# Loading the last 224 rows of w_out: five 108-partition chunks by transfers over three DMA engines, in place of nine 44-partition chunks over eight, five, three and three

## The chip, the cores and the metric

The kernel runs on one core of a Trainium2 chip. A core has five engines that run side by side: TensorE (PE in the profile, its weight loads PEld), VectorE (DVE), ScalarE (ACT), GpSimd (POOL) and SyncE (SP), which issues most transfers. Sixteen DMA engines move the data between the chip's main memory and the on-chip memory of 128 partitions. The metric is the device time of one execution in microseconds (us); lower is better. Times below are medians over several runs; a profile describes one execution.

## What is computed

A decode step of one token for four sequences: layer normalization, then attention over a cache of 4,096 positions in 32 heads, and beside it a gated feed-forward branch, both added to the input. Cut to what matters:

```python
B, Sq, D = 4, 1, 640;  H, Sk, Dh = 32, 4096, 128;  Fh = 864     # bf16
x = A_x
xn = _layernorm(x)
# A: attention over the cache
q = (xn @ wq).reshape(B, Sq, H, Dh).transpose(0, 2, 1, 3)
p = softmax(einsum('bhqd,bhkd->bhqk', q, k_cache) * Dh ** -0.5)
A = einsum('bhqk,bhkd->bhqd', p, v_cache).transpose(0, 2, 1, 3).reshape(B, Sq, H * Dh) @ wo
# B: gated feed-forward
z = gelu(xn @ w_in)                        # w_in: 640 x 1728
z1, z2 = z[..., :Fh], _layernorm(z[..., Fh:])
g = w_sp * z2 + b_sp                       # S = 1: two scalars
Bout = (z1 * g) @ w_out                    # w_out: 864 x 640
return x + A + Bout
```

The two caches are 134 MB each and are read once. All weights together are about 14 MB.

## The kernel before

One large tile, `kv`, holds five slots of equal size, and nearly everything that comes from main memory goes through them. A unit is one (head group, sequence) pair of K or of V: 128 partitions x 65,536 bytes, 8 MB, over two half slots. There are 16 units of K and 16 of V. `seq` gives their order (four K first, then V and K by turns), `place` their slots. SP issues them with `load_unit` (L167) one unit ahead of the computation; a load waits until the slot's earlier readers are done.

Before the units SP issues, in this order: wq (L111), w_in (L114), the first part of w_out (L118) and the rest of w_out (L128). ScalarE's queue issues three tiny ones, w_sp, b_sp (L107, L108) and x (L105). Each transfer raises a counter when it lands; there are eight counters, used in turn in the order of the program, so the ninth transfer of the program waits until the first has landed, and so on. Here the transfers in order are w_sp, wq, b_sp, x, w_in, w_out, and then the small ones.

W_out has 864 rows of 640 bf16 values. The first `nf = FA * P` = 512 rows lie in `kv` as four chunks of 128 partitions. The other 352 rows lie in two tiles of the pool `ktpool`, `w_rest0` with seven chunks and `w_rest1` with two, on 44 partitions (`NRP`). They come in four transfers, listed in `RB` as (partition block of 32, first chunk, i, chunks): 32 partitions with 7 rows each, 20 with 1, 12 with 7 and 12 with 2. `w_rest1` is cleared first (L123, GpSimd), because its partitions aren't all loaded. In the two small tiles' transfers the outer dimension of the source is i (8, 5, 3 and 3). The pool `ktpool` has two buffers, which the transposed K tiles `kT` use later.

The branch B at the start: L287 makes q from wq; L309 and L312 make z, the first part into `z_ps`, the rest into `zr_ps`; ScalarE's L318 and L322 apply gelu and put z in the order of the chunks; L335 to L352 normalize and gate it; L353 transposes it to `uT`, one block of 32 columns for each chunk; and L367 multiplies chunk after chunk with w_out and adds the products to `proj`, where the attention's output joins them later (L517).

The loop over the units: `emit_K` transposes K in 32x32 blocks on VectorE (L389, eight pieces per unit) and multiplies with the zero-padded query (L400). After four units `softmax` follows, and `z_fill` lays the probabilities out for V. `emit_V` multiplies with V (L474, 64 matmuls per unit). At the end wo's last parts are loaded (L175), the last piece of wo in four cuts, and L517 to L583 finish the projection, add the partial sums and store.

Python runs all loops when the program is built, and the Tile framework puts the waits in. Within each engine the instructions run in the order written out.

Of the kernel before, what the change touches and what calls it, by code (L numbers as in the profile page):

```python
# [11 lines left out]
F32 = mybir.dt.float32  # L12
BF16 = mybir.dt.bfloat16
# [3 lines left out]
def kernel(  # L17
# [19 lines left out]
    nc = tc.nc  # L37
    P = 128
    B, Sq, D = A_x.shape
    _, H, Sk, Dh = A_k_cache.shape  # L40
    assert Sq == 1 and B == 4 and Dh == P and D % P == 0
    DC = D // P
# [6 lines left out]
    TC = 32  # L49
# [4 lines left out]
    G = HG * B  # L54
    F2 = B_w_in.shape[1]
    Fh = F2 // 2
    FA = 4
    FR = 9
    RB = ((0, 0, 8, 7), (0, 7, 5, 1), (1, 0, 3, 7), (1, 7, 3, 2))
    NRP = 44  # L60
    assert Fh == FA * P + 4 * sum(i * c for _, _, i, c in RB)
    FC = FA + FR
    NOUT = A_wo.shape[1]
    NH = 2
    NO2 = NOUT // NH
# [3 lines left out]
    const = ctx.enter_context(tc.tile_pool(name="const", bufs=1))  # L69
    small = ctx.enter_context(tc.tile_pool(name="small", bufs=2))  # L70

    NKT = max(2 * TC * 32, 7 * NOUT // 2)
    ktpool = ctx.enter_context(tc.tile_pool(name="ktpool", bufs=2))
    ppool = ctx.enter_context(tc.tile_pool(name="ppool", bufs=2))
    ps_s = ctx.enter_context(tc.tile_pool(name="ps_s", bufs=1, space=bass.MemoryType.PSUM))
# [7 lines left out]
    def misc_ps(shape, dtype):  # L83
        misc_ctr[0] += 1
        return ps_m.tile(shape, dtype, tag="misc", name=f"misc{misc_ctr[0]}")
# [5 lines left out]
    def at_slot(i, n, off=0):  # L91
        return kv[:, i * SL + off:i * SL + off + n]
# [22 lines left out]

    nf = FA * P
    w_out = at_slot(2, FA * NOUT, n_in).rearrange("p (c n) -> p c n", c=FA)
    nc.sync.dma_start(out=w_out, in_=B_w_out[0:nf, :].rearrange("(p c) n -> p c n", p=P))  # L118
    w_rest = []
    for k, n in ((0, 7), (1, 2)):  # L120
        t = ktpool.tile([P, NKT], F32, tag="kT", name=f"w_rest{k}")[:NRP].bitcast(BF16)[:, 0:n * NOUT]
        w_rest.append(t.rearrange("p (c n) -> p c n", c=n))
    nc.gpsimd.memset(w_rest[1].rearrange("p c n -> p (c n)").bitcast(F32), 0.0)  # L123
    r_at = [nf]
    for q, c0, ni, n in RB:
        r_at.append(r_at[-1] + 4 * ni * n)
        k = c0 // 7
        nc.sync.dma_start(out=w_rest[k][32 * q:32 * q + 4 * ni, 0:n].rearrange("p c n -> p (c n)"),  # L128
                          in_=B_w_out[r_at[-2]:r_at[-1], :].rearrange("(r i c) n -> i r (c n)", r=4, c=n))

    NB = 32 * FC
    z_at = n_in + FA * NOUT

# [18 lines left out]
    def unit(item, t0, t1):  # L152

        s0, s1 = place[item]
        assert s1 == s0 + 1 or t1 <= T // 2 or t0 >= T // 2
        if t0 >= T // 2:
            return at_slot(s1, (t1 - t0) * Dh, t0 * Dh - SL)
        return at_slot(s0, (t1 - t0) * Dh, t0 * Dh)
# [47 lines left out]
    xnT = const.tile([P, DC, 32], BF16)  # L206
# [43 lines left out]
    for q in range(4):  # L250
        nc.gpsimd.tensor_copy(out=SelE[32 * q:32 * q + 32, :, q % 2, :],
                              in_=b8[32 * q:32 * q + 32, 8:8 + HP, None].to_broadcast((32, HP, P // HG)))
# [10 lines left out]
                          in_=ident_f[:].rearrange("p (q x c) -> p q x c", q=2, c=C2))  # L263
# [12 lines left out]
    for hf in range(NH):  # L276
        nc.tensor.matmul(proj[0:32, 0:NO2], lhsT=ident_bf[:XR, 1 - hf:33 - hf],
                         rhs=x_bf[:, hf * NO2:(hf + 1) * NO2], start=(hf == 0), stop=False)
# [4 lines left out]
    for hf in range(2):  # L283
        for c in range(DC):
            for j in range(NG):
                n0 = j * HG * Dh + hf * 512
                nc.tensor.matmul(q4_ps[32 * j:32 * j + 32, hf * 512:hf * 512 + 512], lhsT=xnT[:, c, :],  # L287
                                 rhs=wq[:, c, n0:n0 + 512], start=(c == 0), stop=(c == DC - 1))
# [13 lines left out]

    w_z = w_in.rearrange("p c (a f) -> p c a f", a=2)
    z_ps = misc_ps([P, 2, FA, 32], F32)
    zr_ps = misc_ps([64, 2, 256], F32)
    w_za = w_z[:, :, :, 0:nf].rearrange("p c a (q j i) -> p c q a i j", q=4, j=32)
    for c in range(DC):
        for q in range(4):
            nc.tensor.matmul(z_ps[32 * q:32 * q + 32], lhsT=xnT[:, c, :], rhs=w_za[:, c, q], start=(c == 0), stop=(c == DC - 1))  # L309
        for q in range(2):  # L310
            f0, f1 = r_at[2 * q], r_at[2 * q + 2]
            nc.tensor.matmul(zr_ps[32 * q:32 * q + 32, :, 0:f1 - f0], lhsT=xnT[:, c, :],  # L312
                             rhs=w_z[:, c, :, f0:f1], start=(c == 0), stop=(c == DC - 1))
    z_f = at_slot(2, 2 * 3 * NB, z_at).bitcast(F32).rearrange("p (a n) -> p a n", a=3)
    z_b = at_slot(2, 2 * NB, z_at + 6 * NB).rearrange("p (a n) -> p a n", a=2)
    zT = z_f[:, 0:2, :].rearrange("p a (i j) -> p a i j", j=32)
    nc.gpsimd.memset(z_f[:, 0:2, :], 0.0)
    nc.scalar.activation(out=zT[:, :, 0:FA, :], in_=z_ps[:], func=ACT.Gelu_apprx_tanh)  # L318
    for (q, c0, ni, n), f0, f1 in zip(RB, r_at[:-1], r_at[1:]):
        f0, f1 = f0 - r_at[2 * q], f1 - r_at[2 * q]  # L320
        for a in range(2):
            nc.scalar.activation(out=zT[32 * q:32 * q + 32, a, FA + c0:FA + c0 + n, 0:4 * ni].rearrange("p c (i r) -> p c i r", r=4),  # L322
                                 in_=zr_ps[32 * q:32 * q + 32, a, f0:f1].rearrange("p (r i c) -> p c i r", r=4, c=n),
                                 func=ACT.Gelu_apprx_tanh)

    one_bf = const.tile([1, P], BF16)
# [34 lines left out]
    for f0 in range(0, FC, 4):  # L361
        for hf in range(NH):
            for fc in range(f0, min(f0 + 4, FC)):
                n = P if fc < FA else NRP
                nb = 32 if fc == 1 and hf == 0 else RW
                u0, r0 = 32 * fc + 1 - hf, 32 * (fc % 2)
                nc.tensor.matmul(proj[r0:r0 + nb, 0:NO2], lhsT=uT[:n, u0:u0 + nb],  # L367
                                 rhs=(w_out[:, fc] if fc < FA else w_rest[(fc - FA) // 7][:, (fc - FA) % 7])[:, hf * NO2:(hf + 1) * NO2],
                                 start=(fc == 1 and hf == 0), stop=False)


# [9 lines left out]
    def emit_K(u, k):  # L381
# [5 lines left out]
        kw = unit(("k", u), t0, t0 + 2 * TC).bitcast(F32).rearrange("p (t w) -> p t w", w=KW)[:, :, 32 * kh:32 * kh + 32]  # L387
        kT = ktpool.tile([P, NKT], F32, tag="kT", name="kT")[:, 0:2 * TC * 32]
        nc.vector.transpose(kT[:].rearrange("p (t r) -> p t r", r=32), kw)  # L389
# [171 lines left out]
    for c, hf in ((0, 0), (1, 0), (0, 1), (1, 1), (2, 0), (2, 1)):  # L561
        p = min(c, 1)
# [49 lines left out]
```

## Time and profile before

| what | value |
|---|---|
| time, median of 3 runs (663.18 to 663.21) | 663.18 us |
| span of the profiled execution | 661.2 us |
| TensorE busy | 287.5 us, 43% |
| VectorE busy | 372.2 us, 56% |
| ScalarE busy | 73.6 us, 11% |
| GpSimd busy | 67.0 us, 10% |
| read from main memory | 282.24 MB, 427 GB/s over the span |
| packets of the DMA queues | 6930 |

The span counts from the first instruction of the program to the last; what the time holds besides is 2.0 us. An engine is busy while it works on data; waiting and issuing transfers don't count. In the DMA part of the page each digit is the busy share of one fortieth of the span, in tenths. The queue q1 is SP's, q10 ScalarE's; q8 and q14 fetch instructions. The chain of waits goes from the last instruction backwards, at each step to what released it.

The issues of the transfers around the change, with sizes and the median time from issue to landing:

```profile
kv<-in_A_wq_dram SPq DMA_DIRECT2D x1, 5120.0 KB
...
kv<-in_B_w_in_dram SPq DMA_DIRECT2D x1, 2160.0 KB, 19.8
...
kv<-in_B_w_out_dram SPq DMA_DIRECT2D x1, 640.0 KB, 20.9
...
w_rest<-in_B_w_out_dram SPq DMA_DIRECT2D x1, 280.0 KB
...
w_rest<-in_B_w_out_dram SPq DMA_DIRECT2D x1, 105.0 KB
w_rest<-in_B_w_out_dram SPq DMA_DIRECT2D x1, 30.0 KB
w_rest<-in_B_w_out_dram SPq DMA_DIRECT2D x1, 25.0 KB
```

And SP's own timeline up to the first loads of K (start, duration, what):

```profile
1.62 0.46 SPq L118 DMA_DIRECT2D kv<-in_B_w_out_dram  x1
2.12 14.46 SPq L128 DMA_DIRECT2D w_rest<-in_B_w_out_dram  x4
16.62 37.98 SPq L167 DMA_DIRECT2D kv<-in_A_k_cache_dram  x3
```

### The profile page before, as it was taken

To read this page: it belongs to the slowest core of one execution; us is meant where nothing else is said; L and a number is where in the kernel's file an instruction comes from. 1 tells how busy PE (TensorE), PEld (TensorE's weight loads), DVE (VectorE), ACT (ScalarE), POOL (GpSimd) and SP (SyncE) were. 2 spreads that over 40 slices of the span, in tenths; PEclk is the share of its full clock that TensorE was granted. 3 is DMA by queue.
4 is the path that set the end of the run, shared out by engine and by line. 5 is a ranking of instruction groups with operands and counts; after the bars stand their busy time and mean duration, and the time that the engine had idled before them with its cause. 6 is when DMAs were issued, how large, how long until landed. Compare 5 with 4: busy or idle time off the path is not lost.

```text
span 661.2 us, 5415 instructions
## 1 busy us (share of the span) xinstructions
PE 287.5 (43%) x2247; PEld 106.6 (16%) x2247; DVE 372.2 (56%) x306; ACT 73.6 (11%) x145; POOL 67.0 (10%) x137
## 2 busy tenths in 40 slices
PE   0436656446062555235436065533706244551236
PEld 0211212112011121111112022110202112120113
DVE  2229999766191759718356286764629175971112
ACT  0300000341100000430200000070110000043200
POOL 3600000031200000130300000030110000003300
PEclk9857788669577587676758577875858769766678
DMA  9999999999999999999999999999999999999996
GB/s 372 452 446 420 420 447 438 429 444 417 436 436 433 428 425 437 433 436 445 416 432 433 432 421 450 427 432 429 437 440 433 424 433 416 445 444 429 419 420 285
DMA packets 6930, 282.58 MB, mean 427 GB/s; under 512 B 811, under 2 KB 1091, under 8 KB 1487
## 3 DMA queue, kind: packets, MB, share of 16 engines
q1 hardware_dynamic: 6879, 282.24, 99.0%
q8 instruction: 17, 0.28, 0.2%
q14 instruction: 6, 0.05, 0.0%
q10 hardware_dynamic: 28, 0.01, 0.0%
HBM read 282.24 MB, written 0.01 MB: 427 GB/s over the span
## 4 chain that ended last, share of the span: by engine, by line
DMA 77%; DVE 9%; issue 8%; PE 4%; ACT 0%; SPq 0%; DVEq 0%; ACTq 0%
DMA kv<-in_A_k_cache_dram 46%; DMA kv<-in_A_v_cache_dram 26%; DVE kT L389 8%; PE O L474 4%; DMA kv<-in_A_wo_dram 4%; DMA kv<-in_A_wq_dram 2%; DVE pT_t L456 0%; ACT Zb L437 0%; DVE m L407 0%; ACT p_bf L450 0%; PE S L400 0%; PE misc L411 0%; SPq L128 0%; PE proj L517 0%; DVE o_q L569 0%
## 5 line engine op out<-in xcount | busy, mean ns | idle before, releaser
L389 DVE STREAM_TRANSPOSE kT<-kv 128x2048 f32<-128x2048 f32 x128 | 282.8, 2275 | 128.1 <-DMA kv<-in_A_k_cache_dram 128.1
L400 PE MATMUL S<-kT,QZ 128*32 128x512 bf16 x1024 | 187.1, 498 | 261.9 <-DVE kT L389 261.9
L400 PEld LDWEIGHTS <-QZ 128*32 128x32 bf16 x1024 | 59.8, 110 | 387.5 <-issue 323.2
L474 PE MATMUL O<-kv,Zb 128*32 128x512 bf16 x1024 | 75.0, 458 | 56.4 <-DMA kv<-in_A_v_cache_dram 49.5
L437 ACT ACTIVATE Zb<-pT_t,MkE 32x128 bf16<-32x128 bf16 x120 | 60.8, 507 | 117.6 <-PE O L474 104.6
L483 DVE TENSOR_TENSOR om<-O,Mk 128x512 f32<-128x512 f32 x15 | 10.4, 692 | 93.8 <-PE O L474 93.8
L435 POOL TENSOR_SCALAR Zb<-pT_t,MkE 32x128 bf16<-32x128 bf16 x60 | 43.1, 718 | 138.6 <-PE O L474 126.1
L474 PEld LDWEIGHTS <-Zb 128*32 128x32 bf16 x1024 | 34.0, 113 | 97.3 <-issue 69.6
L450 ACT ACTIVATE p_bf<-S,negmax 128x1024 bf16<-128x1024 f32 x4 | 4.5, 1115 | 403.7 <-DVE negmax L417 403.7
L433 DVE TENSOR_SCALAR Zb<-pT_t,MkE 32x128 bf16<-32x128 bf16 x76 | 25.1, 330 | 2.3
L375 POOL COPY QZ<-qT 32x32 bf16<-32x32 bf16 x16 | 5.0, 315 | 188.9 <-PE S L400 188.4
L484 DVE TENSOR_REDUCE R<-om 128x128 f32<-128x512 f32 x15 | 15.3, 1021 | 0.5
L456 DVE STREAM_TRANSPOSE pT_t<-p_bf 128x1024 bf16<-128x1024 bf16 (+1 forms) x8 | 9.6, 1240 | 5.5 <-ACT p_bf L450 5.5
L461 POOL TENSOR_SCALAR rs<-MkB,rowsum 128x4 f32<-128x4 f32 x4 | 1.2, 299 | 112.7 <-ACT p_bf L450 112.7
L507 POOL MEMSET oT<- 128x66 bf16 x4 | 0.5, 146 | 96.6 <-PE proj L517 96.6
L407 DVE TENSOR_REDUCE m<-S 128x1 f32<-128x1024 f32 x4 | 4.9, 1224 | 6.0 <-PE S L400 6.0
L486 DVE TENSOR_SCALAR R<-O,Mk 128x128 f32<-128x128 f32 x1 | 0.3, 350 | 14.0 <-PE O L474 14.0
L496 PE MATMUL misc<-R,SelX 128*128 128x512 f32 x8 | 4.5, 644 | 7.2 <-DVE R L484 5.5
L287 PE MATMUL q<-kv,xnT 128*32 128x512 bf16 x40 | 4.3, 614 | 6.4 <-DVE xnT L208 6.4
L463 PE MATMUL misc<-rs,SelE 128*128 128x4 f32 x8 | 2.4, 365 | 10.4 <-POOL rs L461 10.4
L191 DVE CAST kv<-kv 8x640 f32<-8x640 bf16 x1 | 0.5, 482 | 10.7 <-DMA kv<-in_A_x_dram 10.7
L499 DVE TENSOR_TENSOR om<-misc,h 128x512 f32<-128x512 f32 x4 | 2.8, 692 | 4.9 <-PE misc L496 4.9
(102 smaller groups left out, 80.0 us busy)
## 6 DMA issues: line engine op xcount, KB each, us to landing
kv<-in_A_k_cache_dram SPq DMA_DIRECT2D x8, 4096.0 KB, 30.5
kv<-in_A_v_cache_dram SPq DMA_DIRECT2D x1, 6144.0 KB
kv<-in_A_wq_dram SPq DMA_DIRECT2D x1, 5120.0 KB
kv<-in_A_wo_dram SPq DMA_DIRECT2D x3, 1280.0 KB
kv<-in_B_w_in_dram SPq DMA_DIRECT2D x1, 2160.0 KB, 19.8
kv<-in_A_v_cache_dram SPq DMA_DIRECT2D x1, 2048.0 KB
kv<-in_B_w_out_dram SPq DMA_DIRECT2D x1, 640.0 KB, 20.9
kv<-in_A_wo_dram SPq DMA_DIRECT2D x1, 640.0 KB
```

What stands on the lines that cost most here:

```text
L375: nc.gpsimd.tensor_copy(out=QZ[r0:r0 + 32, :, :, :, 8 + 8 * hp], in_=qT[32 * g:32 * g + 32, NE * hp:NE * hp + NE].rearrange("p e a b -> p ...
L389: nc.vector.transpose(kT[:].rearrange("p (t r) -> p t r", r=32), kw)
L400: nc.tensor.matmul(S_ps[32 * q:32 * q + 32, i], lhsT=QZ[:, b, 2 * kh + w, e, w0:w0 + 32], rhs=kb[:, i, :, e, :, w], start=(b == 0 and k < ...
L407: nc.vector.tensor_reduce(out=m1[:], in_=S_ps[:].rearrange("p i t m -> p (i t m)"), axis=AX.X, op=ALU.max)
L433: nc.vector.tensor_scalar(out=dst, in0=src, scalar1=mk, scalar2=None, op0=ALU.mult)
L435: nc.gpsimd.tensor_scalar(out=dst, in0=src, scalar1=mk, scalar2=None, op0=ALU.mult)
L437: nc.scalar.activation(out=dst, in_=src, func=ACT.Copy, scale=mk)
L450: nc.scalar.activation(out=p_bf[:, M:M + NP], in_=S_ps[:].rearrange("p i t m -> p (i t m)"), func=ACT.Exp, bias=negmax[:, 0:1], scale=scal ...
L456: nc.vector.transpose(pT_t[:, j0:j1, :], blocks)
L474: nc.tensor.matmul(O_ps[32 * q:32 * q + 32, :, :], lhsT=Zb[b % 2][:, w].rearrange("p h c -> p (h c)"), rhs=vv[:, w * 4 * Dh:(w + 1) * 4 * ...
L483: nc.vector.tensor_tensor(out=om4[:], in0=O_ps[:], in1=Mk4[:, :, None].to_broadcast((P, 4, Dh)), op=ALU.mult)
L484: nc.vector.tensor_reduce(out=R, in_=om4[:].rearrange("p c d -> p d c"), axis=AX.X, op=ALU.add)
```

## The change

Five chunks of w_out (640 rows, 800 KB) now come in the 128-partition transfer, in place of four. The other 224 rows are one tile, `w_rest`, with five chunks. 192 rows come in four transfers, one for each block of 32 partitions: 12 partitions with 4 rows (5,120 bytes) each, with an outer dimension of 3 in the source. The last 32 rows come in a fifth transfer, one row on each of 32 partitions, into the fifth chunk. The first four chunks are multiplied over 108 partitions, of which 48 hold rows and the others zeros from the memset (and zeros in `uT`), the fifth over 32. The memset now clears the whole tile, 108 x 1600 fp32 words in place of 44 x 640, and runs before all five transfers.

The order of z in `zr_ps` follows: one matmul for each of the five pieces in each of the five chunks of D, and two gelu activations for each piece, ten in place of eight. The z branch has 10 blocks of 32 columns in place of 13, and L367 has 20 matmuls in place of 26. The `kT` tiles shrink to what K needs, and `w_rest` takes one of the pool's two buffers. The bytes moved are the same.

```diff
-    FA = 4
-    FR = 9
-    RB = ((0, 0, 8, 7), (0, 7, 5, 1), (1, 0, 3, 7), (1, 7, 3, 2))
-    NRP = 44
-    assert Fh == FA * P + 4 * sum(i * c for _, _, i, c in RB)
+    FA = 5
+    FR = 5
+    RB = tuple((q, 0, 4, 3, 4) for q in range(4)) + ((0, 4, 1, 32, 1),)
+    NRP = (108, 108, 108, 108, 32)
+    assert Fh == FA * P + sum(r * i * c for _, _, r, i, c in RB)
...
-    NKT = max(2 * TC * 32, 7 * NOUT // 2)
+    NKT = 2 * TC * 32
...
-    w_rest = []
-    for k, n in ((0, 7), (1, 2)):
-        t = ktpool.tile([P, NKT], F32, tag="kT", name=f"w_rest{k}")[:NRP].bitcast(BF16)[:, 0:n * NOUT]
-        w_rest.append(t.rearrange("p (c n) -> p c n", c=n))
-    nc.gpsimd.memset(w_rest[1].rearrange("p c n -> p (c n)").bitcast(F32), 0.0)
+    w_rest = ktpool.tile([P, NKT], F32, tag="kT", name="w_rest")[:NRP[0]].bitcast(BF16)[:, 0:FR * NOUT]
+    w_rest = w_rest.rearrange("p (c n) -> p c n", c=FR)
+    nc.gpsimd.memset(w_rest.rearrange("p c n -> p (c n)").bitcast(F32), 0.0)
     r_at = [nf]
-    for q, c0, ni, n in RB:
-        r_at.append(r_at[-1] + 4 * ni * n)
-        k = c0 // 7
-        nc.sync.dma_start(out=w_rest[k][32 * q:32 * q + 4 * ni, 0:n].rearrange("p c n -> p (c n)"),
-                          in_=B_w_out[r_at[-2]:r_at[-1], :].rearrange("(r i c) n -> i r (c n)", r=4, c=n))
+    for q, c0, nr, ni, n in RB:
+        r_at.append(r_at[-1] + nr * ni * n)
+        nc.sync.dma_start(out=w_rest[32 * q:32 * q + nr * ni, c0:c0 + n].rearrange("p c n -> p (c n)"),
+                          in_=B_w_out[r_at[-2]:r_at[-1], :].rearrange("(r i c) n -> i r (c n)", r=nr, c=n))
...
-    zr_ps = misc_ps([64, 2, 256], F32)
+    zr_ps = misc_ps([P, 2, 80], F32)
+    z_cols = [(r_at[4] - r_at[3]) * (k // 4) for k in range(len(RB))]
...
-        for q in range(2):
-            f0, f1 = r_at[2 * q], r_at[2 * q + 2]
-            nc.tensor.matmul(zr_ps[32 * q:32 * q + 32, :, 0:f1 - f0], lhsT=xnT[:, c, :],
-                             rhs=w_z[:, c, :, f0:f1], start=(c == 0), stop=(c == DC - 1))
+        for k, (q, *_) in enumerate(RB):
+            f0, f1 = r_at[k], r_at[k + 1]
+            nc.tensor.matmul(zr_ps[32 * q:32 * q + 32, :, z_cols[k]:z_cols[k] + f1 - f0], lhsT=xnT[:, c, :],
+                             rhs=w_z[:, c, :, f0:f1], start=(c == 0 and k < 4), stop=(c == DC - 1 and 0 < k))
...
-                n = P if fc < FA else NRP
+                n = P if fc < FA else NRP[fc - FA]
...
-                                 rhs=(w_out[:, fc] if fc < FA else w_rest[(fc - FA) // 7][:, (fc - FA) % 7])[:, hf * NO2:(hf + 1) * NO2],
+                                 rhs=(w_out[:, fc] if fc < FA else w_rest[:n, fc - FA])[:, hf * NO2:(hf + 1) * NO2],
```

More of the change, by code (lines that the diff above doesn't have):

```diff
@@ L318 @@
     nc.scalar.activation(out=zT[:, :, 0:FA, :], in_=z_ps[:], func=ACT.Gelu_apprx_tanh)
-    for (q, c0, ni, n), f0, f1 in zip(RB, r_at[:-1], r_at[1:]):
-        f0, f1 = f0 - r_at[2 * q], f1 - r_at[2 * q]
+    for k, (q, c0, nr, ni, n) in enumerate(RB):
+        f0, f1 = z_cols[k], z_cols[k] + nr * ni * n
         for a in range(2):
-            nc.scalar.activation(out=zT[32 * q:32 * q + 32, a, FA + c0:FA + c0 + n, 0:4 * ni].rearrange("p c (i r) -> p c i r", r=4),
-                                 in_=zr_ps[32 * q:32 * q + 32, a, f0:f1].rearrange("p (r i c) -> p c i r", r=4, c=n),
+            nc.scalar.activation(out=zT[32 * q:32 * q + 32, a, FA + c0:FA + c0 + n, 0:nr * ni].rearrange("p c (i r) -> p c i r", r=nr),
+                                 in_=zr_ps[32 * q:32 * q + 32, a, f0:f1].rearrange("p (r i c) -> p c i r", r=nr, c=n),
                                  func=ACT.Gelu_apprx_tanh)
```

## The prediction

> **What bounds the kernel now.** I read the page first, then the chain of waits, then the timeline of the start and of the end, and last the trace's DMA records (packets with start, length and bytes; the instants at which each transfer's counter was raised). The page:
>
> ```profile
> span 661.2 us, 5415 instructions
> ...
> DMA  9999999999999999999999999999999999999996
> ...
> q1 hardware_dynamic: 6879, 282.24, 99.0%
> q8 instruction: 17, 0.28, 0.2%
> q14 instruction: 6, 0.05, 0.0%
> ...
> DMA 77%; DVE 9%; issue 8%; PE 4%; ACT 0%; SPq 0%; DVEq 0%; ACTq 0%
> ```
>
> The DMA row never falls below 9 before the last slice, and SP's queue q1 fills 99.0% of 16 engines' span. Two small queues carry instructions on the same engines; they matter below. The chain of waits, in order of time:
>
> ```profile
> 0.71 15.13 DMA kv<-in_A_wq_dram
> 15.84 0.02 issue
> 15.86 0.72 SPq L128
> 16.58 0.04 issue
> 16.62 28.44 DMA kv<-in_A_k_cache_dram
> ...
> 633.07 23.45 DMA kv<-in_A_wo_dram
> ```
>
> DMA feeds DMA from 0.71 us to 656.52. The 28.44 us from the first K issue to its landing are queueing more than transport: in the packet records K's first packet starts at 21.26, right behind w_out. So a change at the start acts through the work each of the 16 engines has in line, not through the instruction that issues it. The end, in the timeline:
>
> ```profile
> 656.56 0.44 PE L517 MATMUL proj<-kv,oT 128*8 128x320 bf16 x4 [0.30 <-DMA kv<-in_A_wo_dram]
> ...
> 657.11 1.37 PE L517 MATMUL last<-kv,oT 128*32 128x160 bf16 x18
> ...
> 658.57 0.32 DVE L580 TENSOR_TENSOR o_bf<-last,o_q 64x160 bf16<-64x160 f32 x1
> ```
>
> The last pieces of wo land at 656.52, 657.32, 657.74 and 658.13, and the last matmuls and additions follow within 0.5 us. The time is the instant at which the most loaded engine finishes, plus 3.1 us of tail (658.13 to 661.2).
>
> **How late each engine is.** A 16-engine transfer raises its counter 16 times, once per engine. At w_out's landing 15 raises lie within 0.29 us and one is 0.94 late. At the first K they lie, after the earliest (41.00): six at 0 to 0.17, one at 0.85, six at 1.32 to 1.59, three at 3.24, 3.42 and 4.06. Between them came only the four small transfers, which raised 8, 5, 3 and 3 times. A packet of 8,960 bytes took 338 ns, of 1,280 55, of 2,560 102 and of 5,120 196, and the next starts at its end. Old rows: three engines 4x338 + 4x55 + 4x338 + 4x102 = 3.33 us; two more 1.57; three more 1.35; eight none. That is the pattern of 3, 5 and 8, with one of the eight moved into the middle: at 40.57 a 16 KB instruction packet ran, and that engine's next K packet ended 1.4 us late.
>
> These delays are never made up, since each engine always has its next transfer in line. Comparing the 16 raises from load to load, each of q8's 17 packets puts one engine back by 1.35 to 1.55 us, and the levels moved repeat after eight: packets 9 to 16 hit the engines of 1 to 8 (six of the eight unloaded ones, two of the five), and packet 17, at 647.59, the engine of packets 1 and 9, one of the eight, a third time. The DVE's 8 KB packets hit one engine of the five three times (about +0.95 each). At the last wo piece the lateness, worked out so, is:
>
> ```
> class                 engines  lateness in us, last wo piece
> all four small ones   3        3.09  3.61  3.77
> one or two of them    5        1.17  1.77  and three of the top four
> none                  8        0  0.63  2.74  2.75  2.77  2.85  2.90  and one of the top four
> the top four                   4.10  4.10  4.16  4.17
> ```
>
> **The change, part by part.** *Packets per engine.* W_out's first part grows from 4 to 5 chunks: eight packets of 5,120 bytes (1.57 us) become eight of 6,400 (no row; 5,120 bytes went at 26.1 bytes per ns and 8,960 at 26.5, so 241 to 245 ns; 243 is taken, 1.94 us in all). Four transfers give three engines 16x196 = 3.14 us, and the 32 rows give every engine 2x55 = 0.11. New minus old, w_out included:
> - the three: 1.94 + 3.14 + 0.11 - 1.57 - 3.33 = +0.29
> - the two: 2.05 - 3.14 = -1.09; the next three: 2.05 - 2.92 = -0.87
> - the eight: 2.05 - 1.57 = +0.49
>
> The two ends of the new packet's cost move all four together by 0.02 either way. Added to the table: the three end at 3.38 to 4.06, the five's top at about 3.1 to 3.3, seven of the eight at 0.49 to 3.39, and the engine hit three times at 4.59 to 4.66. The old end was 4.17. **Sum: +0.42 to +0.49 us, taken as +0.46.**
>
> [...] With free fetches the three would end last before and after, and the sum would be +0.29.
>
> [...]
>
> *SP's queue.* Five small issues in place of four. By the built program's waits the first waits for POOL's memset, the fourth for the counter wq used (15.84), the fifth and K for those of b_sp and x, raised by 10.62. An L128 issue took 719 to 881 ns, so K goes out at about 17.4 instead of 16.62. Cover: the engines have w_in and w_out to move until 21.3. wq's issue at 0.71 led to a first packet at 1.73, so anything before about 20.3 is free. Later loads go out 6 us or more ahead (at 189.54 for engines free from 195.89), and keep their order.
>
> The covers that the next three parts lean on, from the timelines of POOL, TensorE and VectorE:
>
> ```profile
> 1.28 0.62 POOL L123 MEMSET w_rest<- 44x640 f32 x1
> ...
> 12.88 1.24 POOL L197 TENSOR_TENSOR kv<-kv 8x640 f32<-8x640 f32 x1 [9.88 <-DVE kv L196]
> ...
> 36.49 2.83 PE L367 MATMUL proj<-w_rest,kv 44*8 44x320 bf16 x18
> ...
> 45.25 17.66 DVE L389 STREAM_TRANSPOSE kT<-kv 128x2048 f32<-128x2048 f32 x8 [10.00 <-DMA kv<-in_A_k_cache_dram]
> ```
>
> *POOL.* The memset grows from 44x640 to 108x1600. 640, 832 and 1024 elements took 0.62, 0.79 and 0.95 us; by that slope 1.44, so +0.82. SP waits until 2.7 instead of going at 2.12, behind 14 us of wq. POOL then sat idle for 9.88 us before L197, which covers it; uncovered it would cost 0.82.
>
> *TensorE, ScalarE, POOL in the z branch.* L312 goes from 10 to 25 matmuls, narrower; 30 matmuls of both lines took 2.35 us, about 0.08 each, so +1.2 at most. L322 goes from 8 to 10 activations (1.23 us for 8): +0.3. The 128x416 elementwise work shrinks to 128x320: POOL's 4.4 us by about 1.0. L367 goes from 26 to 20 matmuls, 0.9 less. Near zero in sum; cover: L367 ended at 39.3, and DVE sat idle until 45.25 for K (10.00 us). Nobody waits for that branch but L167's third load, which waits for K's transposes (54.15) in any case. Uncovered, it would cost 1.5 us. The first kT tile no longer shares its buffer with w_rest: worth nothing, as K is later.
>
> *Instruction stream.* TensorE gets 19 instructions more. Packets came every 256; the last at record 4357 of 4533, so the next would be due at about 4613, and the new total is 4552: none is added. The last comes about ten matmuls, 1 us, earlier.
>
> **The rivals.**
> 1. *The engine hit three times isn't one of the eight* (it is read off levels 0.05 us apart). Then all four at the top belong to the five and fall by 0.87 or more, and the three end last: 3.77 + 0.29 = 4.06, so 0.11 less than before: 663.07. That is also the floor: the engine that was last at K's landing is one of the three, 3.77 late at the end, and no arrangement here unloads it. For: the two engines of packets 12 and 13 ended at the same level. Against: packet 1 ran exactly when the earliest of the eight was free.
> 2. *An eighteenth instruction packet*: on the engine of packets 2 and 10, 2.74 to 2.90 + 0.49 + 1.5 = 4.7 to 4.9, so +0.56 to +0.72: 663.8 to 663.9. Against: the 61 records missing.
> 3. *Slower, K's issue comes late*: if the fifth small transfer's wait is held until w_in's counter (20.96), K goes out after two issues, at 22.4, its first packet comes at 23.4 in place of 21.7, and the eight idle 1.7 us on top of the sum: 665.3. It decides from an issue at about 20.3. For: the fourth is already held by wq. Against: the wait list.
> 4. *The change doesn't do what it says*: if the four transfers spread over more engines, the eight get up to 0.59 more: 664.2. Against: two old transfers of 12 partitions with a count of 3 raised exactly three times.
>
> **How the numbers follow.** The profiled execution has 661.2 us of span; the median of the runs is 663.18, 2.0 more, which lies outside the span and is left as it is. Likeliest case, 0.62: 663.18 + 0.46 = 663.64. Rival 1: 0.20; rival 2: 0.06; rival 3: 0.05; rival 4: 0.04; a gain nothing here explains: 0.03. A measurement of this kernel tells about 0.2% from no change, 1.33 us, so the likeliest case and rivals 1 and 2 count as no difference, rival 3 as slower, rival 4 mostly as none. Faster 0.03 (the floor in rival 1 excludes it), same 0.89, slower 0.08. The range goes from rival 1 with 0.05 us of spread to rival 2's upper end: 663.0 to 663.95. The likeliest case's own range is 663.5 to 663.75.
>
> **What would show it.** Right: at K's landing three raises about 3.1 us behind the rest, plus what an instruction packet adds, and no group of five in the middle; K's first packet near 21.7; at the last wo piece one raise alone at the end, about 0.5 us behind the next; q8 still with 17 packets; landing near 658.6. Wrong: three raises together at the end (rival 1), 18 packets (rival 2), a gap in the packets before K (rival 3), more than three raises for a small transfer (rival 4).

## The result, and the profile after

| | before | after |
|---|---|---|
| median of 8 runs each | 663.25 us (663.06 to 665.75) | 665.81 us (665.37 to 667.22) |
| ratio, 95% interval | | 1.0034 [1.0022, 1.0045] |
| span of the profiled execution (its own time) | 661.2 us (663.18) | 663.5 us (667.22) |
| the 16 raises of wo's last piece | 653.96 to 658.13 | 656.19 to 660.40 |

The medians differ by 2.56 us, where 0.46 was forecast. The ratio is taken over all runs and not from the two medians; two of the eight executions before were longer than the rest, 664.78 and 665.75 us. The execution that was profiled afterwards has an unusually large rest outside its span (3.7 us; about 2.0 in the seven others), so the two profiles are compared by their spans, which differ by 2.3 us, and by the landing of the last piece of wo, which moved by 2.27. The profiled span after is itself 0.2 us below the median of the eight, 663.7.

The page of the kernel after:

```profile
span 663.5 us, 5437 instructions
...
DMA  9999999999999999999999999999999999999996
...
q1 hardware_dynamic: 6892, 282.24, 99.0%
q8 instruction: 17, 0.28, 0.2%
q14 instruction: 7, 0.05, 0.0%
...
DMA 76%; issue 11%; DVE 9%; PE 3%; SPq 0%; DVEq 0%
```

Nothing here seems to have changed. The bytes are the same, the DMA row is as full, and q1's packets fill the same 99.0% of a longer span. That last line is the clue: the same bytes took more engine time, so some packets became slower; no gap opened. The chain of waits, with start, duration and what ran:

```profile
0.71 15.27 DMA kv<-in_A_wq_dram
...
16.00 0.70 SPq L125
16.71 0.04 issue
16.75 0.42 SPq L125
17.17 0.05 issue
17.22 29.61 DMA kv<-in_A_k_cache_dram
...
634.68 24.11 DMA kv<-in_A_wo_dram
```

K was issued at 17.22, 0.60 later than before, and landed at 46.83 in place of 45.06, 1.77 later. The packet records show that the late issue is not the reason: K's first packet started at 21.68, behind w_out, without a gap. The end, in the timeline (start, duration, engine, line, what, idle time before it):

```profile
658.84 0.44 PE L515 MATMUL proj<-kv,oT 128*8 128x320 bf16 x4 [0.28 <-DMA kv<-in_A_wo_dram]
...
659.38 1.36 PE L515 MATMUL last<-kv,oT 128*32 128x160 bf16 x18
...
660.85 0.32 DVE L578 TENSOR_TENSOR o_bf<-last,o_q 64x160 bf16<-64x160 f32 x1
```

These three lines stand 2.27 to 2.28 us later than before, and the tail from the last landing to the end of the span is again 3.1 us. So all of the difference arose before the end. The raises of the 16 engines say where (lateness in us after the earliest):

```
first K   before  41.00 | 0 .01 .04 .11 .14 .17 .85 1.32 1.38 1.43 1.49 1.50 1.59 3.24 3.42 4.06
          after   43.12 | 0 .05 .09 .14 .20 .24 .29 .29 .34 .67 .76 1.11 1.53 3.16 3.55 3.70
last wo   before 653.96 | 0 .63 1.17 1.77 2.74 2.75 2.77 2.85 2.90 3.09 3.61 3.77 4.10 4.10 4.16 4.17
          after  656.19 | 0 .43 .83 .84 2.62 2.69 2.78 2.79 2.85 2.97 2.99 3.17 3.30 3.34 3.51 4.21
```

The pattern is the forecast one: three engines about 3.1 us behind at K, no group of five in the middle, and one alone at the end. But the earliest engine, which carries none of the four transfers, should have been 0.49 later than before, and it is 2.12 later at the first K and 2.23 at the last wo. So that engine lost about 1.6 us beyond the forecast before 43 us, and nothing much after it. The packet records of that stretch, in us per packet, name the place:

```
5,120 bytes, 48 packets, in order of start (4 transfers x 12)
  the first 24: 0.20 to 0.22     the next 7: 0.20 to 0.27     the last 17: 0.35 to 0.42
65,536 bytes (K), in order of start
  the first 13 (from 21.68):  2.89 to 3.90    the next 16 (from 24.57): 2.52 to 3.60    from 28.16: 2.42
before: 8,960 bytes 0.34, 1,280 0.055, 2,560 0.10, 5,120 0.20, K 2.42, each of them without exception
```

The third and fourth transfer, 24 of the 48 packets, wrote partitions 64 to 75 and 96 to 107. The first 7 of them still took 0.20 to 0.27 us, the other 17 about twice the normal time, and the packets that the other 13 engines had in hand became slow as well. The K packet that started at 22.86, for example, lasted 3.90, so it alone lost 1.48 us by 26.76. Summed over the K packets that started before 32 us, the excess over 2.42 is 23.2 us, 1.45 if it is spread over 16 engines. But three of the sixteen were still busy with the small transfers. The records don't name the engine of a packet, but an engine's next packet starts where its last one ended (in the kernel before, one engine's packets of 8,960 bytes started about 334 ns apart and took 338 ns each); followed in this way, each of the 13 engines with K lost 1.6 to 1.8 us in its first two packets, which is the 1.6 of the earliest engine. The windows view shows the same by its bytes (from:to, length, busy time of the five engines, granted clock, mean DMA share, GB/s); before, then after:

```profile
core 0: us, PE busy (x) PEld busy (x) DVE busy (x) ACT busy (x) POOL busy (x), PEclk, DMA share, GB/s
16.00:40.00 24.00, 11.21 (x99) 5.14 (x100) 5.97 (x14) 6.43 (x15) 13.50 (x40) 0.76 1.05 451
```

```profile
16.00:40.00 24.00, 10.80 (x108) 4.89 (x109) 5.93 (x14) 6.70 (x17) 12.79 (x42) 0.77 1.02 409
```

The DMA engines were busy all the time in both, and moved 451 GB/s before and 409 after. A packet of K is 65,536 bytes, so a window's edge shifts the figure by a few per cent; the direction is to be read here, the size from the packets.

The covers held. The lines below are from the timelines of SyncE, GpSimd, TensorE and VectorE after:

```profile
2.73 14.44 SPq L125 DMA_DIRECT2D w_rest<-in_B_w_out_dram  x5
...
1.28 1.42 POOL L121 MEMSET w_rest<- 108x1600 f32 x1
...
13.13 1.24 POOL L194 TENSOR_TENSOR kv<-kv 8x640 f32<-8x640 f32 x1 [9.34 <-DVE kv L193]
...
36.60 2.04 PE L365 MATMUL proj<-w_rest,kv 108*8 108x320 bf16 x7
...
46.85 13.28 DVE L387 STREAM_TRANSPOSE kT<-kv 128x2048 f32<-128x2048 f32 x6 [11.89 <-DMA kv<-in_A_k_cache_dram]
```

The memset took 1.42 us (1.44 forecast), SP waited until 2.73, GpSimd still idled 9.34 us after it, L365 was done at 38.64, and VectorE waited 11.89 us for K.

### The profile page after: what moved, and what is told of

It is laid out like the page before. It is cut to its first block, busy times and chain, and to the rows that moved or that the text cites. A ratio compares the mean times of both kernels' runs of the same rounds, so it can differ in the third digit from the quotient of the medians.

```text
span 663.5 us, 5437 instructions
## 1 busy us (share of the span) xinstructions
PE 282.9 (43%) x2256; PEld 105.8 (16%) x2256; DVE 371.7 (56%) x306; ACT 74.0 (11%) x147; POOL 66.9 (10%) x137
## 4 chain that ended last, share of the span: by engine, by line
DMA 76%; issue 11%; DVE 9%; PE 3%; SPq 0%; DVEq 0%
DMA kv<-in_A_k_cache_dram 55%; DMA kv<-in_A_v_cache_dram 15%; DVE kT L387 9%; DMA kv<-in_A_wo_dram 4%; PE O L472 3%; DMA kv<-in_A_wq_dram 2%; PE S L398 0%; SPq L125 0%; PE proj L515 0%; DVE o_q L567 0%; DVE o L563 0%; DVEq L387 0%; SPq L172 0%; DVE o_bf L578 0%; SPq L164 0%
## 5 line engine op out<-in xcount | busy, mean ns | idle before, releaser
L398 PE MATMUL S<-kT,QZ 128*32 128x512 bf16 x1024 | 183.5, 490 | 266.3 <-DVE kT L387 266.3
L515 PE MATMUL proj<-kv,oT 128*8 128x320 bf16 x54 | 5.2, 335 | 1.5 <-DMA kv<-in_A_wo_dram 1.5
```

The lines of the kernel that those rows point to most:

```text
L398: nc.tensor.matmul(S_ps[32 * q:32 * q + 32, i], lhsT=QZ[:, b, 2 * kh + w, e, w0:w0 + 32], rhs=kb[:, i, :, e, :, w], start=(b == 0 and k < ...
L515: nc.tensor.matmul(dst[0:nb, 0:n1 - n0], lhsT=state[("oT", g)][:, c0:c0 + nb], rhs=wo_t[g][:, c, n0:n1], start=start, stop=stop)
```

## The experiments

The observation to explain: of the 24 packets to partitions 64 to 75 and 96 to 107, 17 took 0.35 to 0.42 us in place of 0.20, and K's first packets beside them 2.52 to 3.90 in place of 2.42. A 128-partition load raises its counter 16 times and each of the four transfers three times. No record names the engine or the partitions of a packet, so which engine fills which partitions of a large load is not shown. Theories: it is the upper half of the partitions that these three engines reach slowly (A in the expectations); or the place doesn't matter, and the rows, or number, size or order of the transfers do (B); or it is any place that another engine fills in the large loads, a foreign one (C). Which places those are was the author's estimate; the runs compare places. All variants keep the changed kernel's transfers (four of 61,440 bytes over three engines, then 32 rows over sixteen), except e2, which starts from the kernel before. Their `RB` has an offset within the block of 32 partitions as second entry, then first chunk, rows, i and chunks; where two transfers would share partitions, the second pair gets chunks of its own in a second tile, which makes nine small chunks instead of five (e1, e3, e5, e6 and e8; not e4).

| run | partitions of the four transfers | median, us | ratio to before, 95% | slow 5,120 packets | excess of K's packets, sum / 16, us | lost by each of the 13 engines with K, us |
|---|---|---|---|---|---|---|
| after | 0, 32, 64, 96 (12 each) | 665.81 | 1.0034 [1.0022, 1.0045] | 17 of 48 | 1.45 | 1.6 to 1.8 |
| e1_low | 0, 32, 0, 32 | 664.12 | 1.0007 [0.9998, 1.0015] | 0 | 0.04 | 0.0 |
| e3_one_high | 0, 32, 64, 32 | 664.89 | 1.0018 [1.0009, 1.0027] | 9 | 0.69 | 0.8 to 0.9 |
| e5_all_high | 64, 96, 64, 96 | 667.25 | 1.0059 [1.0043, 1.0075] | 36 | 2.79 | 2.8 to 3.3 |
| e4_offset12 | 0, 32, 12, 44 | 665.78 | 1.0037 [1.0027, 1.0047] | 17 | 1.35 | 1.5 to 1.6 |
| e8_offset8 | 0, 32, 8, 40 | 665.56 | 1.0030 [1.0020, 1.0040] | 18 | 1.41 | 1.6 to 1.7 |
| e6_offset4 | 0, 32, 4, 36 | 664.58 | 1.0016 [1.0007, 1.0026] | 5 | 0.39 | twelve 0.3, one 1.7 |
| e2_before_high | before, the 3rd and 4th at 64 | 664.92 | 1.0023 [1.0011, 1.0034] | (8,960 bytes: 8 of 44) | 1.37 | 1.5 to 1.6 |
| e7_fewer_pe | as e1_low | 663.16 | 0.9996 [0.9988, 1.0005] | 0 | 0.13 | 0.1 |

A packet is counted as slow from 0.30 us (8,960 bytes: from 0.4). The last column leaves out what instruction packets add. In e7 each engine lost 0.1 although its transfers lie as in e1; the reason wasn't looked for, so a tenth of a microsecond is not to be read from these columns. The kernel before had a median of 663.31 beside e1 to e4, 663.31 beside e5 to e7 and 663.23 beside e8. The ratios are again taken over all runs and come out up to 0.06% below those of the medians.

**e1_low: the third and fourth transfer back on partitions 0 to 11 and 32 to 43.**

```diff
...
-    RB = tuple((q, 0, 4, 3, 4) for q in range(4)) + ((0, 4, 1, 32, 1),)
-    NRP = (108, 108, 108, 108, 32)
...
+    RB = ((0, 0, 0, 4, 3, 4), (1, 0, 0, 4, 3, 4), (0, 0, 5, 4, 3, 4), (1, 0, 5, 4, 3, 4), (0, 0, 4, 1, 32, 1))
+    NRP = (44, 44, 44, 44, 32, 44, 44, 44, 44)
...
```

> The changed kernel, with the same five transfers of the same rows, but all four three-engine transfers go to partitions 0-11 and 32-43 (more chunks, two tiles); nothing lies on partitions 64 and up. Theory A (writing to partitions 64-107 from the three engines disturbs the engines that fill those partitions): the packets of 5,120 bytes all take about 196 ns, the first K packets 2.42 us, and the time is that of the kernel before plus 0.4 to 0.6 us, about 663.7. Theory B (the rows read, or four such transfers in a row beside K, whatever the destination): packets of 0.4 us and first K packets of 3 to 3.9 us as in the changed kernel, 665.4 to 666.0. [...]

Every one of the 48 packets took 0.20 us, K's packets 2.42 to 2.44, and the median fell by 1.69 us against the changed kernel. The same window as above:

```profile
16.00:40.00 24.00, 11.60 (x109) 4.74 (x109) 6.02 (x14) 6.69 (x17) 13.75 (x40) 0.78 1.04 447
```

447 GB/s in place of 409: the rate of the kernel before is back, with the same number, size and order of transfers. The place decides; e8 below has the same second tile and is slow, so the tile isn't what helps. This kernel is also the experiment that shows the forecast sum by itself, and it is taken up below.

**e2_before_high: the kernel before, with its third and fourth transfer moved up.** It has none of the other edits; what goes with the place is that the first tile is cleared too and that z's order follows.

```diff
-    RB = ((0, 0, 8, 7), (0, 7, 5, 1), (1, 0, 3, 7), (1, 7, 3, 2))
-    NRP = 44
+    RB = ((0, 0, 8, 7), (0, 7, 5, 1), (2, 0, 3, 7), (2, 7, 3, 2))
+    NRP = 76
...
```

> The kernel before, with its third and fourth small transfers (12 partitions, three engines) sent to partitions 64-75 in place of 32-43 (and the first tile cleared too). Theory A: the three engines' last four packets of 8,960 bytes take about 0.7 us in place of 338 ns, the 2,560 ones 0.2, K's packets beside them run at about half speed for 3.5 us, and the time rises by 1.6 to 2.0 us to about 665.0. Theory B: as the kernel before, 663.2 to 663.3.

The last packets of 8,960 bytes took 0.65 to 0.69 us in place of 0.34, those of 2,560 bytes 0.19 to 0.22 in place of 0.10, and K's up to 3.96; each engine with K lost 1.5 to 1.6 us and the time rose by 1.61. So the loss comes with the place alone, without five chunks, the large memset or the fifth transfer.

**e3_one_high and e5_all_high: one transfer, and all four, on the upper partitions.** In e3 the entry `(2, 0, 0, 4, 3, 4)` takes the place of e1's third; e5's first four are:

```diff
+    RB = ((2, 0, 0, 4, 3, 4), (3, 0, 0, 4, 3, 4), (2, 0, 5, 4, 3, 4), (3, 0, 5, 4, 3, 4), (0, 0, 4, 1, 32, 1))
```

> The changed kernel with one of the four transfers on partitions 64-75, the others on 0-11 and 32-43. Theory A: half of the changed kernel's slow stretch (about 1.5 us in place of 3.0), time between the two, about 664.5. Theory B: as the changed kernel, 665.4 to 666.0.

> The changed kernel with all four three-engine transfers on partitions 64-75 and 96-107. If the loss goes by the bytes that an engine writes into partitions which another engine fills (theory C): twice the changed kernel's slow stretch, about 6 us of packets at 0.4 us, K's packets beside them at about half speed, so about twice 1.5 us lost over e1's 664.1: 667 to 667.5. If two such transfers already cost all there is (one block of partitions after the other, or a loss per K load and not per byte): as the changed kernel, 665.8.

One transfer cost each engine with K 0.8 to 0.9 us, two 1.6 to 1.8 (after), four 2.8 to 3.3, and with e1 as the base the medians rose by 0.77, 1.69 and 3.13: the cost goes with the bytes that are written there, about 0.8 us for each 61,440. The slow packets lag behind their cause: in the changed kernel the first one to three of each engine's eight packets there kept nearly their speed, and in e3 four of the nine slow ones, counted off along each engine, belong to the fourth transfer, which was back on 32 to 43.

**e4_offset12: the same kernel as after, with the third and fourth transfer on partitions 12 to 23 and 44 to 55.** These lie in the lower half.

```diff
-    RB = tuple((q, 0, 4, 3, 4) for q in range(4)) + ((0, 4, 1, 32, 1),)
+    RB = ((0, 0, 0, 4, 3, 4), (1, 0, 0, 4, 3, 4), (0, 12, 0, 4, 3, 4), (1, 12, 0, 4, 3, 4), (0, 0, 4, 1, 32, 1))
```

> [...] Theory A (only the half from 64 on): no slow stretch, about 663.7. Theory C (any foreign partition): the slow stretch as in the changed kernel, 665.4 to 666.0. Theory B: the same as C.

As slow as the changed kernel: 17 of 48 packets at 0.34 to 0.41, K's up to 3.95, 1.5 to 1.6 us lost by each engine with K, 665.78. Its row of the windows view reads like the one after:

```profile
16.00:40.00 24.00, 11.07 (x108) 4.59 (x109) 5.72 (x14) 6.69 (x17) 12.62 (x40) 0.74 1.02 409
```

The theory of the upper half falls. Theory C is not refuted, but which engine fills 12 to 23 and 44 to 55 in K's load is not shown.

**e6_offset4 and e8_offset8: shifted by 4 and by 8.** A transfer's 12 partitions are three pieces of four, by the outer dimension of 3 in the source. In e1 all of them lie on 0 to 11 and 32 to 43, where none of the 48 packets was slow; in e4 the third and fourth transfer lie outside of that with all three pieces. Shifted by 4, to 4 to 15 and 36 to 47, each of the two has one piece outside (12 to 15, 44 to 47); shifted by 8, to 8 to 19 and 40 to 51, two. The edit of e6, against e1:

```diff
-    RB = ((0, 0, 0, 4, 3, 4), (1, 0, 0, 4, 3, 4), (0, 0, 5, 4, 3, 4), (1, 0, 5, 4, 3, 4), (0, 0, 4, 1, 32, 1))
+    RB = ((0, 0, 0, 4, 3, 4), (1, 0, 0, 4, 3, 4), (0, 4, 5, 4, 3, 4), (1, 4, 5, 4, 3, 4), (0, 0, 4, 1, 32, 1))
```

> [...]

> [...]

e6: five packets at 0.39 to 0.43, all of them on one engine, and one of the three engines alone 5.09 late at the first K (the other two 3.26 and 3.28). One engine with K had packets of 3.05 and 3.46 and lost 1.7 us; the other twelve had 2.62 and 2.5 and lost 0.3. So with one piece outside, one of the three engines was slow and the other two stayed at 0.20 to 0.24, and one of the 13 engines with K bore the most. Whether these two wrote to the same partitions is not shown. The time, 664.58, is 0.46 above e1's. But the disturbance is not additive: with two pieces outside each of the 13 engines lost 1.6 to 1.7 us, no less than with three (1.5 to 1.8), and the sum of K's excess over 16 was 1.41 us, where e6 had 0.39 and e4 1.35. In e8 the three engines had 5, 6 and 7 slow packets, so all three were slow there, where e6 had one.

**e7_fewer_pe: e1_low with some 208 TensorE instructions fewer.** It bears on another step, the engine that instruction packets hit a third time.

```diff
-        for c in range(DC):
+        for c in range(1):
...
-    for c in range(DC):
+    for c in range(1):
...
-    for f0 in range(0, FC, 4):
+    for f0 in range(0, 4, 4):
...
-                    emit_proj(g - 1)
+                    pass
```

> e1 with some 208 TensorE instructions left out (q and z from the first of five chunks of D only, w_out's product over its first four chunks only, the first head group's output product left out; all loads stay). The instruction packet that comes 17th, at 635.46 in e1, then comes at about 654, after most of its engine's data. Theory (the third instruction packet on one engine is what makes that engine last, as the prediction's table says): the last raise no longer stands alone, the last landing is about 1 us earlier (658.0), the time 663.0 to 663.2. Rival (that engine is late for another reason): as e1, 664.1.

In e1 the 17th instruction packet of TensorE came at 635.46 and left its engine 4.51 us late, 1.05 later than the last of the others. In e7 it came at 657.00, too late to delay anything; the last two engines stood at 3.57 and 3.60, and the last piece landed at 658.10 in place of 658.98. The medians differ by 0.96. The third hit on one engine is what ended last in e1, as the prediction's table has it for the changed kernel.

No variant with the whole computation measured below the kernel before, so there is no version to recommend beyond it. e1's interval includes no difference from the kernel before.

## Why the prediction was wrong

**The step that failed** is the price of the four transfers, "Four transfers give three engines 16x196 = 3.14 us", and with it the first packets of K, which were taken to begin at 2.42 us each. The 196 ns came from w_out's 128-partition load, and the kernel before had no slow packet in its small transfers either: those over eight and five engines start at partition 0, both over three engines write 32 to 43, and packets of 8,960 bytes took 0.34 us, of 2,560 0.10. The change puts half of the four transfers' bytes on 64 to 75 and 96 to 107, while K's first packets run. I read the new blocks in `RB` only for their rows, so this price was missing from the sum, and none of the four rivals stood for it. In its place the runs showed 17 of the 48 packets at 0.35 to 0.42 us, K's first packets at up to 3.90, and 1.6 to 1.8 us lost by each engine with K: 1.69 us of the median (after against e1_low). They tie the loss to the place (e1, e2, e4; e8 against e6) and to the bytes (e3, e5). Why these places cost time is not shown, nor how all 13 engines with K come to be slowed.

**The sum without that term** can be checked on e1, which has all edits but the place (and a second tile). Its earliest engine was at 654.47, 0.51 later than before; the forecast for the eight was +0.49. Its last engine was 4.51 late relative to that, where the table has 4.10 to 4.17. The last instruction packet isn't the reason: it moved its engine from about 3.1 to 4.63, 1.5 us, where 1.35 to 1.55 was read. Part of the difference seems to have stood at the first K already, where the engine hit by the first one was 1.80 late and in the kernel before at most 1.59; the rest wasn't traced. So e1 landed at 658.98, 0.85 later than before, and its median is 0.81 above the kernel before, where +0.46 was forecast; the interval over all runs, -0.1 to +1.0 us, holds both values. In the changed kernel itself the last engine was 4.21 late, close to the table. There the forecast 0.49 and the 1.6 to 1.8 lost make 2.1 to 2.3, and the landing moved by 2.27. In the medians 0.81 and 1.69 make 2.50 of the 2.56; the rest is that the kernel before had 663.25 in one series and 663.31 in the other.

**Right:** the classes and signs of the four groups (the group of five gone, three engines about 3.1 behind at K, one alone at the end, 0.7 behind the next where about 0.5 was forecast); 17 instruction packets before the end (in the trace before they came 226 to 320 TensorE records apart, 259 in the mean, where 256 was taken); K's first packet at 21.68 against 21.7; SP's late issue at no cost, 17.22 against 17.4; three raises for each of the four transfers; the covers of the memset and of branch B.

**The rivals.** Rival 1 (another engine hit three times) is refuted by the one late raise at the end; rival 2 by the 17 packets; rival 3 by the issue at 17.22; rival 4 by the three raises (its 0.59 is an estimate, the 48 packets of 5,120 bytes spread over 16 engines, three each at 0.196 us; no run spread them so). Rival 3's number, 665.3, comes near the measured time by luck, with the wrong reason. (Rival 2's lower end is 663.74 by its own sum, not 663.8.) The range, 663.0 to 663.95, didn't hold the time, because it was made of the uncertainties of the terms that I had, and a missing term has none. "These delays are never made up" held: the earliest engine was 2.12 us later than before at 43 us and still 2.23 later at 656.

## What to carry to other kernels

In a kernel whose DMA engines never run empty, price a small transfer by where it writes as well as by its bytes. Here the same four transfers left K's packets at 2.42 to 2.44 us on partitions 0 to 11 and 32 to 43 (e1); with two of them elsewhere, 17 or 18 of the 48 small packets took about twice their 0.20 us and each engine with K lost 1.5 to 1.8 us (after, e4, e8), and much less, 0.3 for twelve of the 13, where one piece in three lay elsewhere (e6). This is shown for one kernel, with loads over 128 partitions beside the small transfers. When a packet's duration is carried over from a row, ask to which partitions it went in that row, what ran beside it, and what will in the new place. And where the busy share stays at its ceiling while the time grows, compare the durations of equal packets: q1 filled 99.0% of the span before and after, while K's packets went from 2.42 us to as much as 3.90.

## What was unexpected of the hardware

With one piece of two small transfers outside 0 to 11 and 32 to 43 (e6), one engine's small packets took 0.39 to 0.43 us in place of 0.20 and one engine's K packet 3.46 in place of 2.42; that all the others slow down with them was not expected. After the change each of the 13 engines with K lost 1.6 to 1.8 us, in a stretch of some three microseconds. One piece outside does little of this (K's packets 2.62 in place of 2.42 on the twelve others), two do it in full (1.6 to 1.7 us on each engine with K in e8). Why two are enough stays open, and so does whether a small transfer with no K beside it would disturb anything, which wasn't tried.

An instruction packet of 16 KB costs the DMA engine that it lands on about 1.5 us (1.35 to 1.55 in the trace before; 1.5 for the last one in e1), and nothing gives it back: in e1 the third one on one engine was worth 0.96 us of the median. With three of them on one engine, a spread of 0.2 us each is as large as the whole forecast.
